# The last block's second half of tokens first, and token factors inside the last additions, in an attention and expert kernel

## The chip, the cores and the metric

The kernel runs on 1 core of one Trainium2 chip. The metric is the device time of one execution in microseconds (us); less is better. A core has a matrix engine (TensorE, PE in the rows; its weight loads are PEld), a vector engine (DVE), a scalar engine (ACT), GpSimd (POOL), and SyncE (SP), which issues transfers. Each runs its own instructions in the order in which they were written, and waits on semaphores for the others.

## What is computed

Three layers, one after the other: an attention with landmarks, a layer of eight experts of which each token takes one, and a layer with a squared ReLU. The change touches the third alone:

```python
def _moe2_ref(x, w_in, w_out):          # x: 4608 tokens x 512; w_in: 512 x 2048; w_out: 2048 x 512
    h = np.maximum(x @ w_in, 0.0)
    return (h * h @ w_out).astype(np.float32)

x = np.ascontiguousarray(attn_out.transpose(0, 2, 1, 3)).reshape(B * S, H * D)
x = _moe_ref(x=x, **moe_kwargs)
return _moe2_ref(x=x, **moe2_kwargs)
```

## The kernel before

The third layer is `phase_m2`. The 4608 tokens go in 18 blocks of `TB` = 256 (`NB` = 18), each in two halves t = 0 and t = 1 of 128 tokens. Tokens lie sorted by expert, so each block has a tile `fa` with a scale factor for each token (`sc[t]`) and the row of the output to which the token belongs.

The hidden width of 2048 is worked through in 8 pairs per block, 144 pairs in all. For one pair, `pair` issues 24 matmuls (lines 1136 to 1138, tile `h2`, shown as h) for two slices of 128 hidden columns. ACT takes the ReLU (line 1141), DVE squares (line 1142) and forms the combinations for a seven-product scheme in place of eight (Strassen's; lines 1143 to 1146), ACT rounds them to float16 (line 1148, `hq[:, 0]`), and after the `yield` DVE writes the rest that the rounding lost (line 1150, `hq[:, 1]`).

`piece(b, f)` then issues 21 matmuls (line 1158): for each of the seven products k, three matmuls (high by high, high by low, low by high), added up in PSUM over the 8 pairs of the block. The seven sums lie two and two in four PSUM tiles, `sums[k // 2][:, k % 2]`; each tile is one bank of PSUM. In the order of k the sums are called p1, p6 (tile o0), p7, p5 (o1), p4, p3 (o2) and p2 (o3).

`result(b)` makes the output of the block from the seven sums: `r[0]` = p1, `r[1]` = p6 + r0, `r[2]` = p7 + r1, the four quarters `o[t][:, z]` by further additions (line 1170, DVE), then for each t a multiplication of 128x512 elements by the token factors (line 1173, ACT, inside `put`) and an indirect DMA that POOL issues (line 1174) and that scatters 128 rows into the output. Both transfers of a block write the tensor `out`, and each waits for the one before.

The order is written out by hand, with a loop over g: at step g the kernel issues `pair` g, then `piece` of pair g - 2 (`LAG` = 2), then, where that piece is the last of a block, `result`, and then what is left of `pair` g (line 1150). So PE alternates between 24 and 21 matmuls, and the 21 matmuls of the next block, which begin the four tiles of sums anew, stand one pair behind `result`.

Of the kernel before, what the change touches and what calls it, by code (L numbers as in the profile page):

```python
# [6 lines left out]
F32 = mybir.dt.float32  # L7
# [3 lines left out]
AF = mybir.ActivationFunctionType  # L11
ALU = mybir.AluOpType
# [1084 lines left out]
TB = 256  # L1097
LAG = 2

PRODS = ((5, 5), (1, 1), (6, 6), (0, 0), (4, 2), (2, 4), (3, 3))  # L1100


def load_block(nc, pool, x2, blk):

    n = TB // 128
    xT = pool.tile([128, 8, TB], F16, tag="x2T", name="x2T")
    for t in range(n):
        r0 = TB * blk + 128 * t
        nc.sync.dma_start_transpose(out=xT[:, :, 128 * t:128 * t + 128], in_=x2[r0:r0 + 128, 0:2 * DM])
    fa = pool.tile([128, n, 4], F16, tag="fa", name="fa", bufs=3)  # L1110
    nc.sync.dma_start(out=fa, in_=x2[TB * blk:TB * blk + TB, 2 * DM:XD].rearrange("(a p) c -> p a c", p=128))
    return xT, fa


def phase_m2(tc, x2, wi, wo, first, out):


    nc = tc.nc
    V, ACT, PE = nc.vector, nc.scalar, nc.tensor
    with (  # L1120
        tc.tile_pool(name="n2", bufs=2, reuse_waits="tile") as n2,
        tc.tile_pool(name="n3", bufs=3, reuse_waits="tile") as n3,
        tc.tile_pool(name="npo", bufs=1, space=PSUM, reuse_waits="tile") as npo,
        tc.tile_pool(name="nph", bufs=4, space=PSUM, reuse_waits="tile") as nph,
    ):
        NB = NT // TB
        NP = 8 * NB
        sums = [npo.tile([128, 2, TB], F32, name=f"o{i}") for i in range(4)]

        def pair(xT, i, s):  # L1130

            ph = nph.tile([128, 2, TB], F32, tag="h2", name="h2")
            for z, f in enumerate((i + 8, i)):
                fs = slice(128 * f, 128 * f + 128)
                for c in range(4):
                    PE.matmul(ph[:, z], wi[:, 0, c, fs], xT[:, c], start=(c == 0), stop=False)  # L1136
                    PE.matmul(ph[:, z], wi[:, 0, c, fs], xT[:, 4 + c], start=False, stop=False)  # L1137
                    PE.matmul(ph[:, z], wi[:, 1, c, fs], xT[:, c], start=False, stop=(c == 3))  # L1138

            q = n3.tile([128, 7, 128], F32, tag="q", name="q")  # L1140
            ACT.activation(q[:, 3:7], ph.rearrange("p z (t n) -> p (z t) n", t=2), AF.Relu, scale=2.0 ** -7)  # L1141
            V.tensor_tensor(q[:, 3:7], q[:, 3:7], q[:, 3:7], op=ALU.mult)  # L1142
            V.tensor_tensor(q[:, 0], q[:, 6], q[:, 4], op=ALU.add)
            V.tensor_tensor(q[:, 6], q[:, 5], q[:, 6], op=ALU.subtract)
            V.tensor_tensor(q[:, 1], q[:, 0], q[:, 5], op=ALU.subtract)
            V.tensor_tensor(q[:, 2], q[:, 3], q[:, 1], op=ALU.subtract)  # L1146
            s["hq"] = hq = n3.tile([128, 2, 7, 128], F16, tag="hq", name="hq", bufs=4)
            ACT.activation(hq[:, 0], q, AF.Copy, scale=0.5)  # L1148
            yield
            V.scalar_tensor_tensor(hq[:, 1], q, 0.5, hq[:, 0], op0=ALU.mult, op1=ALU.subtract)  # L1150

        def piece(b, f):

            hq = ps[8 * b + f]["hq"]
            for k, (a, w) in enumerate(PRODS):
                for i, (u, x) in enumerate(((0, 0), (0, 1), (1, 0))):

                    PE.matmul(sums[k // 2][:, k % 2], hq[:, u, a], wo[:, x, f, w], start=(f == 0 and i == 0 and k % 2 == 0),  # L1158
                              stop=(f == 7 and i == 2), skip_group_check=True)

        def result(b):

            fa = st[b][1]
            sc = [fa[:, t, 0:2].bitcast(F32) for t in range(2)]
            o = [n2.tile([128, 2, TB], F32, tag=f"out{t}", name=f"out{t}") for t in range(2)]
            r = [n2.tile([128, TB], F32, tag=f"r{i}", name=f"r{i}") for i in range(3)]
            p1, p6, p7, p5, p4, p3, p2 = (sums[k // 2][:, k % 2] for k in range(7))

            def add(to, x, y):
                V.tensor_tensor(to, x, y, op=ALU.add)  # L1170

            def put(t):
                ACT.activation(o[t], o[t], AF.Copy, scale=sc[t])  # L1173
                nc.gpsimd.indirect_dma_start(  # L1174
                    out=out, out_offset=bass.IndirectOffsetOnAxis(ap=fa[:, t, 2:4].bitcast(I32), axis=0),
                    in_=o[t].rearrange("p z n -> p (z n)"), in_offset=None)
            ACT.activation(r[0], p1, AF.Copy)  # L1177
            add(r[1], p6, r[0])
            add(r[2], p7, r[1])
            add(o[0][:, 1], p5, r[1])  # L1180
            add(o[1][:, 1], p5, r[2])
            add(o[1][:, 0], p4, r[2])
            put(1)
            add(o[0][:, 1], p3, o[0][:, 1])
            add(o[0][:, 0], p2, r[0])
            put(0)

        st = list(first)
        ps = [{} for _ in range(NP)]
        for g in range(NP + LAG):  # L1190
            rest = iter(())
            if g < NP:
                b, i = divmod(g, 8)
                if i == 0 and len(st) < min(b + 2, NB):
                    st.append(load_block(nc, n2, x2, b + 1))
                rest = pair(st[b][0], i, ps[g])
                next(rest)
            if g >= LAG:
                piece(*divmod(g - LAG, 8))
                if (g - LAG) % 8 == 7:  # L1200
                    result((g - LAG) // 8)
            next(rest, None)


# [8 lines left out]
def moe_kernel(tc, q, k, v, wg, w1, w2, win, wout, out, x_rows, x2):  # L1213
    nc = tc.nc
    with tc.tile_pool(name="cst", bufs=1, reuse_waits="tile") as cp:
# [16 lines left out]
        with (  # L1232
# [4 lines left out]
            with tc.tile_pool(name="mb", bufs=1, reuse_waits="tile") as mb:  # L1237
# [3 lines left out]
                with tc.tile_pool(name="fp", bufs=2, reuse_waits="tile") as fp:  # L1241
                    pend = {}

                    def fill(j):

                        i = j - PT
                        if 0 <= i < 32:
# [3 lines left out]
                            else:  # L1251
# [9 lines left out]
                    phase_m1(tc, cst, x_rows, x2, w1, w2, rt, stg, wb, fill,  # L1261
                             lambda: b0.extend(load_block(nc, x0, x2, b) for b in range(1)))
            phase_m2(tc, x2, wi, wo, b0, out)


# [21 lines left out]
```

## Time and profile before

| | us |
|---|---|
| median of 3 runs | 1443.82 |
| lowest and highest | 1439.42, 1449.20 |
| the profiled execution, its own time | 1445.92 |
| its span, from the first to the last instruction | 1444.20 |
| third layer, from its first sums to the last | about 730 to 1434 |

The span of the profiled execution is 1.7 us shorter than its own time; the rest lies around it. The profiled execution is 2.1 us above the median. In the rows, times are us from the span's start unless a unit stands there; a row of a timeline gives the start, the time taken, and, in brackets, how long the engine was idle before it and what ended that.

### The profile page before, as it was taken

What the parts mean: (1) busy time and instruction counts of PE and PEld (TensorE: products, weight loads), DVE (VectorE), ACT (ScalarE), POOL (GpSimd) and SP (SyncE); (2) the same over time, 40 slices, a digit from 0 to 9 for tenths busy, and PEclk for the clock granted to TensorE, in tenths of its full rate; (3) what the DMA queues carried; (4) which work ended last, traced back from release to release, by engine and by line L of the source; (5) the groups of instructions that cost most, each with busy time, mean ns of one, the idle gap of its engine ahead of it and who ended that gap; (6) DMA issues with size and microseconds to landing.
All of it is one profiled execution on the core that took longest, in us unless ns stands there. A gap on an engine that the chain in (4) does not pass through costs nothing. (4 is left out here: it accounts for less than half of the span.)

```text
span 1444.2 us, 35176 instructions
## 1 busy us (share of the span) xinstructions
PE 1352.3 (94%) x14312; PEld 1077.5 (75%) x14312; DVE 1040.5 (72%) x2651; ACT 575.8 (40%) x979; POOL 274.1 (19%) x282
## 2 busy tenths in 40 slices
PE   5999889889898997899899999999999999999996
PEld 4555555667575775667688888888888888888886
DVE  5888998858888887989556666666666666666664
ACT  4555565333553353443333333333333333333332
POOL 4434563111111223132200000000000000000000
PEclk9999999999999999999999999999999999999999
DMA  8767674476758547364310111111111101111100
GB/s 197 164 162 187 158 175 94 122 190 126 212 119 224 131 123 205 87 132 102 72 33 16 30 31 31 30 23 24 29 30 30 30 19 27 30 31 30 30 9 22
DMA packets 133695, 127.05 MB, mean 88 GB/s; under 512 B 90832, under 2 KB 109264, under 8 KB 133520
## 3 DMA queue, kind: packets, MB, share of 16 engines
q1 hardware_dynamic: 123680, 94.45, 28.5%
q0 software_dynamic: 9200, 30.21, 6.7%
q8 instruction: 114, 1.87, 0.6%
q14 instruction: 61, 0.50, 0.1%
q10 hardware_dynamic: 640, 0.02, 0.0%
HBM read 219.49 MB, written 28.89 MB: 172 GB/s over the span
## 5 line engine op out<-in xcount | busy, mean ns | idle before, releaser
L1158 PE MATMUL o<-wo,hq 128*128 128x256 f16 x3024 | 356.1, 272 | 0.0
L1158 PEld LDWEIGHTS <-hq 128*128 128x128 f16 x3024 | 295.6, 98 | 37.3 <-issue 2.8
L1136 PE MATMUL h<-x2T,wi 128*128 128x256 f16 x1152 | 314.8, 273 | 5.0 <-ACTq L1037 5.0
L1138 PE MATMUL h<-x2T,wi 128*128 128x256 f16 x1152 | 314.7, 273 | 0.0
L1137 PE MATMUL h<-x2T,wi 128*128 128x256 f16 x1152 | 314.7, 273 | 0.0
L1148 ACT ACTIVATE hq<-q 128x896 f16<-128x896 f32 x144 | 136.8, 950 | 289.9 <-DVE q L1146 289.9
L1150 DVE SCALAR_TENSOR_TENSOR hq<-q,hq 128x896 f16<-128x896 f32 x144 | 157.1, 1091 | 129.0 <-ACT hq L1148 129.0
L135 PE MATMUL py<-wb,hT 128*128 128x512 f16 x864 | 202.3, 392 | 22.2 <-DVE ss L153 16.3
L120 PE MATMUL ph<-xT,wb 128*128 128x128 f16 x1152 | 196.9, 220 | 8.7 <-DMA xT<-xh 6.8
L122 PE MATMUL ph<-xT,wb 128*128 128x128 f16 x1152 | 196.9, 220 | 3.4 <-DVE wb L1046 3.2
L121 PE MATMUL ph<-xT,wb 128*128 128x128 f16 x1152 | 196.9, 220 | 0.0
L1174 POOL DMA_INDIRECT out<-out,fa x36 | 54.5, 1514 | 665.3 <-ACT out L1173 590.6
L135 PEld LDWEIGHTS <-hT 128*128 128x128 f16 x864 | 84.9, 101 | 124.0 <-DVE hT L126 18.2
L1142 DVE TENSOR_TENSOR q<-q 128x512 f32<-128x512 f32 x144 | 99.5, 691 | 92.6 <-ACT q L1141 92.6
L1141 ACT ACTIVATE q<-h 128x512 f32<-128x512 f32 x144 | 85.4, 593 | 139.7 <-PE h L1138 139.7
L120 PEld LDWEIGHTS <-wb 128*128 128x128 f16 x1216 | 119.6, 98 | 14.8 <-issue 3.8
L1137 PEld LDWEIGHTS <-wi 128*128 128x128 f16 x1152 | 113.0, 98 | 16.2 <-issue 2.9
L1136 PEld LDWEIGHTS <-wi 128*128 128x128 f16 x1152 | 113.0, 98 | 15.7 <-SPq L1037 2.5
L1138 PEld LDWEIGHTS <-wi 128*128 128x128 f16 x1152 | 113.0, 98 | 13.4
L122 PEld LDWEIGHTS <-wb 128*128 128x128 f16 x1216 | 119.6, 98 | 4.4 <-DVE wb L1046 4.4
L121 PEld LDWEIGHTS <-wb 128*128 128x128 f16 x1216 | 119.6, 98 | 4.0
L126 DVE SCALAR_TENSOR_TENSOR hT<-ph,hT 128x512 f16<-128x512 f32 x72 | 49.7, 690 | 61.0 <-ACT hT L125 31.0
(289 smaller groups left out, 1904.8 us busy)
## 6 DMA issues: line engine op xcount, KB each, us to landing
stg<-in_moe_w SPq DMA_DIRECT2D x76, 2048.0 KB
qn<-in_q SPq DMA_DIRECT2D x16, 576.0 KB
kn<-in_k SPq DMA_DIRECT2D x16, 576.0 KB
vn<-in_v SPq DMA_DIRECT2D x16, 576.0 KB
fw<-in_moe_w_in SPq DMA_DIRECT2D x16, 512.0 KB
fw<-in_moe_w_out SPq DMA_DIRECT2D x16, 512.0 KB
x_rows<-xr SPq DMA_DIRECT2D x32, 192.0 KB
stg<-in_moe_w SPq DMA_DIRECT2D x16, 256.0 KB
```

Source lines behind the costliest of these rows:

```text
L120: nc.tensor.matmul(ph[:, f4], wh[:, c, fs], xT[:, c], start=(c == 0), stop=False)
L121: nc.tensor.matmul(ph[:, f4], wh[:, c, fs], xT[:, 4 + c], start=False, stop=False)
L122: nc.tensor.matmul(ph[:, f4], wl[:, c, fs], xT[:, c], start=False, stop=(c == 3))
L135: self.nc.tensor.matmul(py, hT[:, a, f], w[:, f], start=(i == 0), stop=(i == len(ps) - 1))
L1136: PE.matmul(ph[:, z], wi[:, 0, c, fs], xT[:, c], start=(c == 0), stop=False)
L1137: PE.matmul(ph[:, z], wi[:, 0, c, fs], xT[:, 4 + c], start=False, stop=False)
L1138: PE.matmul(ph[:, z], wi[:, 1, c, fs], xT[:, c], start=False, stop=(c == 3))
L1141: ACT.activation(q[:, 3:7], ph.rearrange("p z (t n) -> p (z t) n", t=2), AF.Relu, scale=2.0 ** -7)
L1142: V.tensor_tensor(q[:, 3:7], q[:, 3:7], q[:, 3:7], op=ALU.mult)
L1148: ACT.activation(hq[:, 0], q, AF.Copy, scale=0.5)
L1150: V.scalar_tensor_tensor(hq[:, 1], q, 0.5, hq[:, 0], op0=ALU.mult, op1=ALU.subtract)
L1158: PE.matmul(sums[k // 2][:, k % 2], hq[:, u, a], wo[:, x, f, w], start=(f == 0 and i == 0 and k % 2 == 0), stop=(f == 7 and i == 2), skip_ ...
```

## The change

In `result`, t = 1 is finished first for every block: the additions of `o[1]` come before anything of `o[0]`, and p5 + r1 goes to a new tile `r[3]`. For t = 0, ACT multiplies `r[3]` and `r[0]` by the token factors (two instructions of 128x256), and the last two additions of DVE become multiply-and-adds that scale p3 and p2 on their way (lines 1188 and 1189). The multiplication of `o[0]` as a whole goes. A `yield` splits `result` ahead of these two.

In the last block alone, pair 143 is issued before piece 4, the pieces 5, 6 and 7 are cut into products 0 to 4 and products 5 and 6, and the second parts of all three (18 matmuls) come after the first half of `result`.

```diff
-        def piece(b, f):
+        def piece(b, f, ks=range(7)):
 
             hq = ps[8 * b + f]["hq"]
-            for k, (a, w) in enumerate(PRODS):
+            for k in ks:
+                a, w = PRODS[k]
...
             def put(t):
-                ACT.activation(o[t], o[t], AF.Copy, scale=sc[t])
                 nc.gpsimd.indirect_dma_start(
...
             add(r[2], p7, r[1])
-            add(o[0][:, 1], p5, r[1])
             add(o[1][:, 1], p5, r[2])
             add(o[1][:, 0], p4, r[2])
+            add(r[3], p5, r[1])
+            ACT.activation(o[1], o[1], AF.Copy, scale=sc[1])
             put(1)
-            add(o[0][:, 1], p3, o[0][:, 1])
-            add(o[0][:, 0], p2, r[0])
+            ACT.activation(r[3], r[3], AF.Copy, scale=sc[0])
+            ACT.activation(r[0], r[0], AF.Copy, scale=sc[0])
+            yield
+            V.scalar_tensor_tensor(o[0][:, 1], p3, sc[0], r[3], op0=ALU.mult, op1=ALU.add)
+            V.scalar_tensor_tensor(o[0][:, 0], p2, sc[0], r[0], op0=ALU.mult, op1=ALU.add)
             put(0)
...
             if g >= LAG:
-                piece(*divmod(g - LAG, 8))
-                if (g - LAG) % 8 == 7:
-                    result((g - LAG) // 8)
+                if g == NP - 2:
+
+                    next(rest, None)
+                    continue
+                if g == NP - 1:
+                    piece(NB - 1, 4)
+                b, f = divmod(g - LAG, 8)
+
+                end = b == NB - 1 and f >= 5
+                piece(b, f, range(5) if end else range(7))
+                if f == 7:
+                    res = result(b)
+                    next(res)
+                    for f in range(5, 8) if end else ():
+                        piece(b, f, (5, 6))
+                    next(res, None)
```

DVE at the end of the block before the last (block 16), before the change. The names out0 and out1 are `o[0]` and `o[1]`, o0 to o3 the four tiles of sums; each row ends with what it waits for (DMASW and DMAHW are transfers).

```order
L1170 TENSOR_TENSOR r1_22462<-o0_14413,r0_22461 128x256 [waits Activation_49]
L1170 TENSOR_TENSOR r2_22463<-o1_14414,r1_22462 128x256 [waits DVE_49,PE_49]
L1170 TENSOR_TENSOR out0_22459<-o1_14414,r1_22462 128x256 [waits DMASW7_49]
L1170 TENSOR_TENSOR out1_22460<-o1_14414,r2_22463 128x256 [waits DMASW6_49,DVE_49]
L1170 TENSOR_TENSOR out1_22460<-o2_14415,r2_22463 128x256 [waits PE_49]
L1170 TENSOR_TENSOR out0_22459<-o2_14415,out0_22459 128x256 [waits DVE_49]
L1170 TENSOR_TENSOR out0_22459<-o3_14416,r0_22461 128x256 [waits PE_49]
L1150 SCALAR_TENSOR_TENSOR hq_22436<-q_22429,hq_22436 128x896
```

The same place on DVE after the change:

```order
L1171 TENSOR_TENSOR r1_22494<-o0_14413,r0_22493 128x256 [waits Activation_49]
L1171 TENSOR_TENSOR r2_22495<-o1_14414,r1_22494 128x256 [waits DVE_49,PE_49]
L1171 TENSOR_TENSOR out1_22492<-o1_14414,r2_22495 128x256 [waits DMASW6_49,DVE_49]
L1171 TENSOR_TENSOR out1_22492<-o2_14415,r2_22495 128x256 [waits PE_49]
L1171 TENSOR_TENSOR r3_22496<-o1_14414,r1_22494 128x256
L1188 SCALAR_TENSOR_TENSOR out0_22491<-o2_14415,fa_21439,r3_22496 128x256 [waits DMAHW4_49,DMASW7_49,Activation_49]
L1189 SCALAR_TENSOR_TENSOR out0_22491<-o3_14416,fa_21439,r0_22493 128x256 [waits PE_49,Activation_49]
L1150 SCALAR_TENSOR_TENSOR hq_22468<-q_22461,hq_22468 128x896
```

The last read of tile o1 moves from the fourth place to the fifth, and the two rows that read o2 and o3 last now wait for ACT.

ACT at the same place, before the change (fa holds the token factors, q and hq belong to the pairs):

```order
L1177 ACTIVATE r0_22461<-o0_14413 128x256 [waits PE_49]
L1173 ACTIVATE out1_22460<-out1_22460,fa_21411 128x512 [waits DMAHW4_49,DMASW6_49,DVE_49]
L1173 ACTIVATE out0_22459<-out0_22459,fa_21411 128x512 [waits DMASW7_49,DVE_49]
L1141 ACTIVATE q_22502<-h2_22477 128x512 [waits PE_49,Activation_49]
L1148 ACTIVATE hq_22509<-q_22502 128x896 [waits DVE_49]
```

And after it:

```order
L1177 ACTIVATE r0_22493<-o0_14413 128x256 [waits PE_49]
L1183 ACTIVATE out1_22492<-out1_22492,fa_21439 128x512 [waits DMAHW4_49,DMASW6_49,DVE_49]
L1185 ACTIVATE r3_22496<-r3_22496,fa_21439 128x256 [waits DVE_49]
L1186 ACTIVATE r0_22493<-r0_22493,fa_21439 128x256 [waits Activation_49]
L1141 ACTIVATE q_22536<-h2_22511 128x512 [waits PE_49]
```

Ahead of the two multiply-and-adds of DVE there now stand the scaling of out1 and of r3, in this order; the second 128x512 scaling is gone.

PE after the change at the end of the last block, where the last piece's product 4 ends and product 5 of piece 5 follows (hq_22802 is that of pair 143, hq_22711 that of pair 141):

```order
L1159 MATMUL o2_14415<-wo_4552,hq_22802 128x256
L1159 LDWEIGHTS hq_22802
L1159 MATMUL o2_14415<-wo_4552,hq_22802 128x256
L1159 LDWEIGHTS hq_22711
L1159 MATMUL o2_14415<-wo_4552,hq_22711 128x256 [waits DVE_49]
L1159 LDWEIGHTS hq_22711
L1159 MATMUL o2_14415<-wo_4552,hq_22711 128x256
```

The 18 matmuls that were moved behind the first half of `result` begin with a wait for DVE; the pieces of the last block before the change have none there.

## Rows read from the trace of the kernel before

**Rows 1.** The page, part 1: busy time of each engine, share, instructions.
```profile
PE 1352.3 (94%) x14312; PEld 1077.5 (75%) x14312; DVE 1040.5 (72%) x2651; ACT 575.8 (40%) x979; POOL 274.1 (19%) x282
```
**Rows 2.** Busy time by stretch: PE, PEld, DVE, ACT, POOL, granted clock, DMA share, GB/s.
```profile
808.00:1399.00 591.00, 591.00 (x5395) 527.42 (x5393) 377.84 (x825) 206.41 (x285) 46.70 (x30) 1.00 0.12 27
```
**Rows 3.** Waits of PE's weight loads, 730 to 1434: us in all, times, longest.
```profile
PEld L1158 <- issue: 2.8, 17, 0.2
```
**Rows 4.** Timeline of PE: the first piece of block 17, in three parts.
```profile
1401.21 0.82 PE L1158 MATMUL o<-wo,hq 128*128 128x256 f16 x6
...
1402.01 0.81 PE L1158 MATMUL o<-wo,hq 128*128 128x256 f16 x6
...
1402.67 0.60 PE L1158 MATMUL o<-wo,hq 128*128 128x256 f16 x4
```
**Rows 5.** Timeline of DVE at the same place: the result of block 16.
```profile
1400.34 0.42 DVE L1170 TENSOR_TENSOR r<-o,r 128x256 f32<-128x256 f32 x1 [1.29 <-ACT r L1177]
...
1400.87 0.42 DVE L1170 TENSOR_TENSOR r<-o,r 128x256 f32<-128x256 f32 x1
1401.21 0.42 DVE L1170 TENSOR_TENSOR out<-o,r 128x256 f32<-128x256 f32 x1
...
1401.54 0.41 DVE L1170 TENSOR_TENSOR out<-o,r 128x256 f32<-128x256 f32 x1
...
1401.87 0.41 DVE L1170 TENSOR_TENSOR out<-o,r 128x256 f32<-128x256 f32 x1
1402.20 0.41 DVE L1170 TENSOR_TENSOR out<-o,out 128x256 f32<-128x256 f32 x1
```
**Rows 6.** Timeline of ACT at the same place.
```profile
1402.32 0.72 ACT L1173 ACTIVATE out<-out,fa 128x512 f32<-128x512 f32 x1 [2.01 <-DVE out L1170]
...
1402.99 0.72 ACT L1173 ACTIVATE out<-out,fa 128x512 f32<-128x512 f32 x1
...
1403.61 0.58 ACT L1141 ACTIVATE q<-h 128x512 f32<-128x512 f32 x1
```
**Rows 7.** Groups by line and shape: busy us, mean ns of one, idle before.
```profile
L1141 ACT ACTIVATE q<-h 128x512 f32<-128x512 f32 x144 | 85.4, 593 | 139.7 <-PE h L1138 139.7
...
L1173 ACT ACTIVATE out<-out,fa 128x512 f32<-128x512 f32 x36 | 24.9, 722 | 36.3 <-DVE out L1170 36.3
...
L1177 ACT ACTIVATE r<-o 128x256 f32<-128x256 f32 x18 | 6.6, 366 | 1.8 <-PE o L1158 1.8
...
L1150 DVE SCALAR_TENSOR_TENSOR hq<-q,hq 128x896 f16<-128x896 f32 x144 | 157.1, 1091 | 129.0 <-ACT hq L1148 129.0
```
**Rows 8.** Timelines of DVE, PEld and ACT at the end of the last block.
```profile
1424.79 1.09 DVE L1150 SCALAR_TENSOR_TENSOR hq<-q,hq 128x896 f16<-128x896 f32 x1 [1.01 <-ACT hq L1148]
1426.82 0.69 DVE L1142 TENSOR_TENSOR q<-q 128x512 f32<-128x512 f32 x1 [0.93 <-ACT q L1141]
...
1430.85 0.22 PEld L1158 LDWEIGHTS <-hq 128*128 128x128 f16 x3 [0.24 <-DVE hq L1150]
...
1431.50 0.38 ACT L1177 ACTIVATE r<-o 128x256 f32<-128x256 f32 x1 [1.83 <-PE o L1158]
...
1433.90 0.72 ACT L1173 ACTIVATE out<-out,fa 128x512 f32<-128x512 f32 x1 [2.01 <-DVE out L1170]
```
**Rows 9.** Timeline of POOL (blocks 16 and 17), and the chain that ended last.
```profile
1403.32 1.47 POOL L1174 DMA_INDIRECT out<-out,fa  x1 [33.73 <-ACT out L1173]
...
1436.37 0.98 POOL L1174 DMA_INDIRECT out<-out,fa  x1 [26.71 <-issue]
1439.88 0.97 POOL L1174 DMA_INDIRECT out<-out,fa  x1 [2.53 <-DMA out<-out,fa]
...
1436.37 2.73 DMA out<-out,fa
```
**Rows 10.** Busy time by stretch, columns as in rows 2: two places before the third layer's sums.
```profile
555.20:558.20 3.00, 0.34 (x2) 0.00 (x0) 2.90 (x9) 1.25 (x2) 0.00 (x0) 1.00 1.22 212
721.10:724.50 3.40, 3.37 (x17) 2.38 (x17) 0.00 (x0) 0.00 (x0) 0.00 (x0) 0.50 0.23 85
```

More of the change, by code (lines that the diff above doesn't have):

```diff
@@ L1165, in result @@
             o = [n2.tile([128, 2, TB], F32, tag=f"out{t}", name=f"out{t}") for t in range(2)]
-            r = [n2.tile([128, TB], F32, tag=f"r{i}", name=f"r{i}") for i in range(3)]
+            r = [n2.tile([128, TB], F32, tag=f"r{i}", name=f"r{i}") for i in range(4)]
             p1, p6, p7, p5, p4, p3, p2 = (sums[k // 2][:, k % 2] for k in range(7))
```

## The prediction

> **What bounds the kernel now.** The page comes first: PE is busy 94% of the span [rows 1]. An average over three layers says little, so the next view is busy time by stretch. From 808 to 1399 us, inside the third layer, PE is busy for all of 591.00 us with 5395 matmuls, 0.1095 us each, at a granted clock of 1.00 [rows 2]: one matmul starts every 0.109 us and nothing else matters as long as PE is fed. The list of waits names the exceptions: 17 times PE's loads for line 1158 were held, 2.8 us in all, 0.165 us each [rows 3]. There are 17 block ends with a block behind them, so every one of them costs a little already, and a block end is the place to read closely. In the first piece of block 17 six matmuls start from 1401.21, the seventh not at 1401.87 but at 1402.01, and the thirteenth at 1402.67 [rows 4]. The seventh opens tile o1 again. It writes the half of p7, which DVE read last in r2 (ended 1401.29), yet it starts 0.06 us after the end, at 1401.95, of the addition that read p5, the other half of that tile [rows 5]. So a piece waits at its 1st, 7th, 13th and 19th matmul for the last reader of a whole tile of sums, and at the seventh this wait decides already: **there is no slack between the result of a block and the next block's sums.** The thirteenth follows the last read of o2 (1402.20 + 0.41 = 1402.61 [rows 5]) by the same 0.06 us, so it has none either.
>
> The Trainium skill, "PSUM — Partial Sum Buffer", section "PSUM bank collisions raise a hardware error", says that an engine which reads a bank while a matmul writes any part of it collides, so software has to keep them apart. The row of the seventh matmul agrees: the half does not count, the tile does.
>
> **The change at the 17 block ends.** The first half of `result` is the same up to r2, which starts at 1400.87. Then the order differs. Before, p5 + r1 needed no r2 and began 0.34 us later; now the first addition of out1 comes next and needs r2, so it starts when r2 has ended and been signalled. From DVE to ACT a signal takes 0.04 us (an addition ends at 1402.28, ACT starts at 1402.32 [rows 5, 6]); I take the same inside DVE: 1400.87 + 0.42 + 0.04 = 1401.33. Independent additions follow each other by 0.33 us [rows 5]: second addition of out1 1401.66 to 1402.07, r3 1401.99 to 1402.40. r3 is now the last reader of o1, so the seventh matmul starts at 1402.46 and not at 1402.01: **0.45 us** later.
>
> For o2, DVE's multiply-and-add of p3 waits for ACT's scaled r3, and ACT does out1 first. ACT starts on out1 at 1402.07 + 0.04 = 1402.11, and the next instruction starts 0.67 us behind a 128x512 one (1402.32, 1402.99 [rows 6]): r3 at 1402.78. How long 128x256 takes from SBUF with a factor per token is in no row. It lies between 0.366 us (that size, from PSUM, no factor) and 0.722 us (twice the size, with the factor); 512 instead of 256 elements from PSUM cost 0.593 - 0.366 = 0.227 us, so I take 0.722 - 0.227 = 0.495 us [rows 7]. It ends at 1403.27, DVE starts at 1403.31. A multiply-and-add of 896 elements takes 1.09 us [rows 7], an addition of 256 takes 0.42 [rows 5]; at one element rate for both that is 0.42 us here: end 1403.73, and the thirteenth matmul at 1403.79, where it was 1402.67. That is **1.12 us** in all, 0.45 of it already waited at the seventh. The nineteenth needs o3: scaled r0 follows on ACT from about 1403.22 to 1403.71, DVE's last multiply-and-add runs 1403.75 to 1404.17, and PE comes to it at 1403.79 + 6 x 0.109 = 1404.44; nothing is added.
>
> Nobody gives this back. PE has no idle time later to absorb it [rows 2]. Behind the waiting DVE instruction stand line 1150 of the pair under way, and behind that the squares of the next pair. Line 1150 moves to about 1404.1 and ends at 1405.2; its hq is read a pair and a piece after 1401.21, some 45 x 0.109 = 4.9 us, so from 1406.1 at the earliest: hidden, with 0.9 us to spare. ACT's line 1141, at 1403.61 [rows 6], comes at about the same time, since one scaling of 128x512 becomes two of 128x256. Where an output leaves costs nothing in the first 17 blocks: POOL idles 33.7 us ahead of the next [rows 9]. Sum: 17 x 1.12 = **+19.0 us**; with 0.366 or 0.722 us for the unknown scaling the thirteenth matmul stands at 1403.66 or 1404.01, 0.99 or 1.34 us late: +16.8 to +22.8.
>
> **The change at the end.** Pair 143 goes ahead of piece 4, 21 x 0.109 = 2.3 us earlier on PE, but its squares stand on DVE behind line 1150 of pair 142, which ends at 1424.79 + 1.09 = 1425.88; line 1142 can come at 1425.87 and not 1426.82, 0.95 us earlier [rows 8]. From there to the end of the last hq nothing changes, and the last piece waited for just that (PEld 1430.85, 0.24 us for line 1150 [rows 8]), so its sums are 0.95 us earlier, and r0 starts at 1430.55 in place of 1431.50. Then r1, r2 and the two additions of out1 as above: r0 + 2.15 us to the end of out1, against 1433.90 - 1431.50 = 2.40 us to ACT's start on it before. ACT starts on out1 at about 1432.73, **1.17 us earlier**. The 18 matmuls moved back must wait for the same addition, since p3 shares a tile with p4: they run from 1432.75 to 1434.9, and out0 is ready at about 1435.4.
>
> That lateness is hidden by POOL. The first transfer began at 1436.37 and landed 2.73 us later, and only then the second started, at 1439.88 [rows 9]. The second start moves with the first, and out0 has until about 1438. In the last block the first transfer began 1.75 us after ACT's end on out1 (1434.62); in block 16 it was 0.28 us (1403.04 to 1403.32) [rows 6, 8, 9]. If the 1.75 stays, the end moves by -1.2 us; with 0.28 by -2.6; if DVE's work beside it stretches POOL's instruction from 0.98 to 1.47 us as in block 16 [rows 9], by -0.7. I take **-1.2**, the nearest row being that of the same transfer.
>
> **Sum.** +19.0 - 1.2 = +17.8 us, bounds 16.8 - 2.6 = +14.2 and 22.8 - 0.7 = +22.1. The profiled execution took 1445.9 us (span 1444.2 and 1.7 around it), so this one would take 1463.7; it lay 2.1 us above the median of the runs, and against 1443.8 the time is **1461.6 us**, 1.2% more.
>
> **Rivals.**
> The block ends cost nothing and only the end of the program is seen: 1443.8 - 1.2 = 1442.6. The mechanism would be slack: PE reaching the seventh and thirteenth matmul after 1402.40 and 1403.73 anyway. It decides if the first piece of the next block came 1.1 us later against DVE. The pause of 0.14 us at 1401.87 and the 17 equal pauses speak against it [rows 3, 4]; for it speaks only that rows of PE are partly modelled. 0.07.
>
> The halves of a tile are waited for apart. Then the seventh goes free after r2, the tenth (p5) waits for r3 until 1402.46 (0.27 us later than 1401.21 + 9 x 0.109), and the sixteenth (p3), before at 1402.67 + 0.33 = 1403.00, starts at 1403.79: 0.79 us, 17 x 0.79 - 1.2 = +12.2, 1456.0. The seventh matmul's row speaks against it. The rule of the Trainium skill's page on PSUM named above would exclude it altogether; by halves the sum would be 1456.0, by whole banks 1461.6. 0.08.
>
> The pauses lower the clock. After a wait of 5.0 us a stretch of 3.4 us ran at 0.50, the level of 1.2 GHz in place of 2.4 [rows 10]. Were that to follow each block end, it would cost about 1.7 us more each, 17 x 1.7 = 29: 1490. The Trainium skill, "TensorE: Matmul & The Clock Gate", Part 1, takes the low clock for the default and activity for what lifts it, which makes such a fall possible. But a stretch at 555 us with two matmuls in 3 us kept 1.00 [rows 10], and pauses of 0.45 and 0.67 us are far shorter. 0.03.
>
> **Chances.** The forecast has 0.80, and 0.02 is left for what I don't see. About 1% (14.4 us) is what a measurement of this kernel can tell from no change: three runs lay between 1439.4 and 1449.2. The forecast lies only 3.4 us beyond that line, so of its 0.80 some 0.13 fall within 1%, and 0.67 are slower; with the clock rival 0.70. The first two rivals are within 1%: 0.07 + 0.08 + 0.13 = 0.28, of which the first could reach -1% by scatter alone; faster 0.02. The range for 8 in 10 takes the bounds (1458 to 1466) with the scatter of a median, and reaches down past the rival of the halves: 1453 to 1468.
>
> **What would show it.** Right: at each of 17 block ends PE pauses about 0.6 us ahead of the seventh matmul of a piece (0.15 before) and about 0.65 us ahead of the thirteenth, ended by DVE, while DVE waits some 0.9 us for ACT in `result`; the list of waits has 20 us on these lines; the first transfer of the last block starts about 1.2 us earlier against the last pair. Wrong: no pause ahead of the thirteenth, or the transfers of the last block not moved, or a granted clock under 1.00 after 735 us.

## The result, and the profile after

| | before | after |
|---|---|---|
| median, lowest to highest, 6 runs each (us) | 1448.12, 1439.42 to 1449.77 | 1465.9, 1462.85 to 1469.94 |
| ratio of after to before, 95% interval | | 1.0136, 1.0111 to 1.0161 |
| profiled execution, its span (us) | 1445.92, 1444.2 | 1466.19, 1464.5 |

The changed kernel is 1.4% slower; 17.8 us had been forecast, the medians differ by 17.8 us, and the spans of the two profiled executions by 20.3 us. The median of before rose from 1443.8 to 1448.1 us when three more runs joined it, so the forecast of 1461.6 us, made against the first three, lies 4.3 us below the median of after for that reason alone. That the 17.8 us of the forecast and those of the medians agree to 0.1 us is luck: the interval of the ratio leaves 16 to 23 us. The traces, added up below, give 19.3 - 1.24 = 18.1 us for the change itself.

The page, part 1, of the kernel after (busy time, share, instructions) tells almost nothing apart from [rows 1]; the work is the same:

```profile
PE 1354.6 (92%) x14312; PEld 1078.6 (74%) x14312; DVE 1045.4 (71%) x2651; ACT 578.2 (39%) x997; POOL 255.5 (17%) x282
```

Only ACT has 18 instructions more, one per block. The list of waits from 730 us to the end (us in all, times, longest) is where to look:

```profile
PEld L1159 <- issue: 23.9, 35, 1.4
...
DVE out L1188 <- ACT r L1185: 14.6, 17, 0.9
PE o L1159 <- DVE out L1188: 9.0, 17, 0.5
PE o L1159 <- DVE r L1171: 7.6, 17, 0.5
```

Before there were 2.8 us in 17 waits of the weight loads and no such wait of PE's matmuls [rows 3]. Now 17 waits end with r (the new last reader of o1) and 17 with the multiply-and-add of p3 (the last reader of o2), and ahead of the second DVE itself waits 17 times, 0.86 us each, for ACT. The weight loads' waits are the same pauses seen from the other side, longer, since a matmul's modelled end hides some 0.17 us of each: 23.9 us now in 35 waits, 1.4 of it at the end of the program.

The timeline of PE at the first piece of block 17, in three parts as in [rows 4], with the idle time ahead in brackets:

```profile
1421.60 0.82 PE L1159 MATMUL o<-wo,hq 128*128 128x256 f16 x6
...
1422.87 0.81 PE L1159 MATMUL o<-wo,hq 128*128 128x256 f16 x6 [0.45 <-DVE r L1171]
...
1424.21 0.38 PE L1159 MATMUL o<-wo,hq 128*128 128x256 f16 x2 [0.53 <-DVE out L1188]
```

The seventh matmul starts 1.27 us behind the first (0.80 before, by the rows) and the thirteenth 2.61 (1.46 before). DVE and ACT at the same place, against [rows 5] and [rows 6]:

```profile
1421.27 0.42 DVE L1171 TENSOR_TENSOR r<-o,r 128x256 f32<-128x256 f32 x1
1421.73 0.42 DVE L1171 TENSOR_TENSOR out<-o,r 128x256 f32<-128x256 f32 x1
...
1422.07 0.41 DVE L1171 TENSOR_TENSOR out<-o,r 128x256 f32<-128x256 f32 x1
1422.40 0.41 DVE L1171 TENSOR_TENSOR r<-o,r 128x256 f32<-128x256 f32 x1
1423.67 0.48 DVE L1188 SCALAR_TENSOR_TENSOR out<-o,fa,r 128x256 f32<-128x256 f32 x1 [0.86 <-ACT r L1185]
1424.07 0.48 DVE L1189 SCALAR_TENSOR_TENSOR out<-o,fa,r 128x256 f32<-128x256 f32 x1
```

```profile
1422.52 0.72 ACT L1183 ACTIVATE out<-out,fa 128x512 f32<-128x512 f32 x1 [1.81 <-DVE out L1171]
1423.15 0.49 ACT L1185 ACTIVATE r<-r,fa 128x256 f32<-128x256 f32 x1
1423.55 0.49 ACT L1186 ACTIVATE r<-r,fa 128x256 f32<-128x256 f32 x1
```

r3 ends at 1422.81 and PE goes on at 1422.87; the multiply-and-add of p3 ends at 1424.15 and PE goes on at 1424.21. Both times 0.06 us lie between, as before the change.

The end of the program, timelines of PE, DVE, ACT and POOL, against [rows 8] and [rows 9]:

```profile
1439.93 0.27 PE L1136 MATMUL h<-x2T,wi 128*128 128x256 f16 x1
...
1451.37 1.59 PE L1159 MATMUL o<-wo,hq 128*128 128x256 f16 x13 [0.25 <-DVE hq L1150]
1454.22 2.13 PE L1159 MATMUL o<-wo,hq 128*128 128x256 f16 x18 [1.27 <-DVE out L1171]
...
1456.53 0.47 DVE L1189 SCALAR_TENSOR_TENSOR out<-o,fa,r 128x256 f32<-128x256 f32 x1
...
1452.01 0.38 ACT L1177 ACTIVATE r<-o 128x256 f32<-128x256 f32 x1 [1.83 <-PE o L1159]
1454.21 0.72 ACT L1183 ACTIVATE out<-out,fa 128x512 f32<-128x512 f32 x1 [1.81 <-DVE out L1171]
...
1456.67 0.98 POOL L1174 DMA_INDIRECT out<-out,fa  x1 [28.71 <-ACT r L1186]
1460.18 0.97 POOL L1174 DMA_INDIRECT out<-out,fa  x1 [2.52 <-DMA out<-out,fa]
```

A yardstick for the end alone is the stretch from pair 142's first matmul, the last thing that is the same in both, to the start of the last transfer. Before, that matmul starts here:

```profile
1418.39 0.27 PE L1136 MATMUL h<-x2T,wi 128*128 128x256 f16 x1
```

That is 1439.88 - 1418.39 = 21.49 us before and 1460.18 - 1439.93 = 20.25 us after: 1.24 us are won, and then the first transfer's landing stands ahead of the second as it did.

**Where the 20.3 us of the spans came from.** For the block ends the yardstick is the first transfer of block 0 and of block 16 on POOL:

```profile
774.02 0.97 POOL L1174 DMA_INDIRECT out<-out,fa  x1 [50.71 <-ACT out L1183]
...
1423.52 0.97 POOL L1174 DMA_INDIRECT out<-out,fa  x1 [36.11 <-ACT out L1183]
```

649.50 us for 16 blocks, 40.59 each; before, 772.03 to 1403.32 is 631.29 us, 39.46 each. So a block end costs 1.14 us more, and 17 of them 19.3 us. The end gives back 1.24. The rest, 2.2 us, arose before the change has any effect: the first matmul of line 1159 starts at 732.8 us, that of line 1158 at 730.6.

### The profile page after: what moved, and what is told of

It reads as the page before. It is cut to its first block, busy times and chain, and to the rows that moved or that the text cites. A ratio compares the mean times of both kernels' runs of the same rounds, so it can differ in the third digit from the quotient of the medians.

```text
span 1464.5 us, 35163 instructions
## 1 busy us (share of the span) xinstructions
PE 1354.6 (92%) x14312; PEld 1078.6 (74%) x14312; DVE 1045.4 (71%) x2651; ACT 578.2 (39%) x997; POOL 255.5 (17%) x282
## 5 line engine op out<-in xcount | busy, mean ns | idle before, releaser
L1159 PE MATMUL o<-wo,hq 128*128 128x256 f16 x3024 | 358.9, 272 | 18.1 <-DVE out L1188 9.0
L1159 PEld LDWEIGHTS <-hq 128*128 128x128 f16 x3024 | 295.6, 98 | 58.4 <-issue 23.9
L1174 POOL DMA_INDIRECT out<-out,fa x36 | 35.6, 989 | 702.2 <-ACT out L1183 626.4
```

## The experiments

The columns of this table are read from the trace of each kernel: the distance of blocks (first transfers of blocks 0 and 16, over 16), the seventh and thirteenth matmul of a block's first piece behind its first, and the stretch from pair 142 to the last transfer. All are taken before rounding, those of the matmuls as medians over the 17 block ends. The last column is the ratio to the kernel before, with its 95% interval; e6, e7 and e8 ran once and have none.

| kernel | distance | seventh | thirteenth | end stretch | ratio |
|---|---|---|---|---|---|
| before | 39.46 | 0.81 | 1.47 | 21.49 | |
| after | 40.59 | 1.27 | 2.61 | 20.25 | 1.0136 (1.0111 to 1.0161) |
| e1_tail_only | 39.45 | 0.80 | 1.46 | 20.25 | 0.9984 (0.9961 to 1.0008) |
| e2_ends_only | 40.59 | 1.26 | 2.60 | 21.27 | 1.0119 (1.0064 to 1.0175) |
| e3_both_orders | 39.52 | 0.80 | 1.53 | 20.25 | 0.9973 (0.9948 to 0.9998) |
| e4_act_order | 40.31 | 1.26 | 2.32 | 20.26 | 1.0096 (1.0067 to 1.0125) |
| e5_dve_order | 40.80 | 0.81 | 2.81 | 20.26 | 1.0166 (1.0119 to 1.0212) |
| e6_split_alone | 39.46 | 0.81 | 1.47 | 21.27 | |
| e7_act_goes_on | 39.46 | 0.81 | 1.47 | 20.26 | |
| e8_pair_alone | 39.46 | 0.81 | 1.47 | 21.14 | |
| e9_pool_goes_on | 39.46 | 0.81 | 1.47 | 20.26 | 1.0018 (0.9993 to 1.0042) |

The theory: PE, which has no slack, waits at each block end for the last reader of a whole tile of sums, and the change makes these readers late. The main rival, once the result was known: the instructions that the change adds cost by themselves, or the cut last block does.

### The two halves of the change apart: e1 and e2

e1_tail_only gives blocks 0 to 16 their old result back and leaves the last block as changed:

```diff
             add(r[2], p7, r[1])
+            if b < NB - 1:
+                add(o[0][:, 1], p5, r[1])
+                add(o[1][:, 1], p5, r[2])
+                add(o[1][:, 0], p4, r[2])
+                ACT.activation(o[1], o[1], AF.Copy, scale=sc[1])
+                put(1)
+                add(o[0][:, 1], p3, o[0][:, 1])
+                add(o[0][:, 0], p2, r[0])
+                ACT.activation(o[0], o[0], AF.Copy, scale=sc[0])
+                put(0)
+                yield
+                return
```

> Blocks 0 to 16 take the old result, block 17 the changed order and the split pieces. Theory (all of the loss is PE held at the 17 block ends by tiles of sums that are read later; the end of the program gains): the distance from one block's first sums to the next goes back from 40.59 to 39.46 us, and the stretch from pair 142's first matmul to the end of the span stays at 24.57 us as after the change (25.81 before): 1.2 us less than before, which is less than a time of the whole can tell. Rival (something else in the changed program, such as the split last block, also costs in every block or before the third layer): distances above 39.46, or a time more than 5 us above before.

The distances are those of before and the end stretch is that of after. The time, 0.9984 of before, is not told apart from no change, as a gain of 1.2 us in 1446 (0.1%) can't be.

e2_ends_only keeps the changed result and takes the cuts and the early pair away:

```diff
-                if g == NP - 2:
-
-                    next(rest, None)
-                    continue
-                if g == NP - 1:
-                    piece(NB - 1, 4)
...
-                end = b == NB - 1 and f >= 5
+                end = False
```

> The changed result in all 18 blocks, the last block's pieces and pair 143 in the old order. Theory: 17 x 1.14 = 19.4 us from the block ends, and of the end's gain only the part that the order of out1 gives (r0 to ACT's start on out1 2.15 to 2.2 us in place of 2.40), about -0.2 us: +19.2 us against before, end stretch 25.6 us. Rival (the slowdown belongs to the split last block): the time of before, distances 39.46.

It has the distances of after and an end stretch 0.22 us below before; its ratio covers both +19.2 us (1.013) and after. So all of the loss sits in the code of `result`, and none in the cut last block.

### The same instructions in another order: e3, e4, e5

All three keep every instruction of the change and the last block as changed. In blocks 0 to 16, e4_act_order moves two lines of ACT, e5_dve_order one line of DVE, and e3_both_orders both, so that it reads:

```diff
             add(r[2], p7, r[1])
+            add(r[3], p5, r[1])
             add(o[1][:, 1], p5, r[2])
             add(o[1][:, 0], p4, r[2])
-            add(r[3], p5, r[1])
-            ACT.activation(o[1], o[1], AF.Copy, scale=sc[1])
-            put(1)
             ACT.activation(r[3], r[3], AF.Copy, scale=sc[0])
             ACT.activation(r[0], r[0], AF.Copy, scale=sc[0])
+            ACT.activation(o[1], o[1], AF.Copy, scale=sc[1])
+            put(1)
             yield
```

> Same instructions as after the change, block 17 in the order of the change; in blocks 0 to 16 DVE adds r3 ahead of out1, and ACT scales r3 and r0 ahead of out1. Theory (what counts is when the last reader of a tile of sums is done, not how many instructions there are): seventh matmul as before; r3 scaled 1.32 to 1.81 us after r1's start, multiply-and-add of p3 ends 2.34 us after r1's start, thirteenth matmul 0.05 to 0.1 us later than before: distance 39.5 to 39.55, about +1 us in 17 ends, with the end's -1.2 about the time of before. Rival (the two more ACT instructions, the 0.06 us longer multiply-and-adds and the wait on ACT cost by themselves): the distance stays near 40.59, +18 us.

Timelines of e3_both_orders at the first piece of block 16, PE and then DVE:

```profile
1362.88 0.82 PE L1159 MATMUL o<-wo,hq 128*128 128x256 f16 x6
1363.69 0.81 PE L1159 MATMUL o<-wo,hq 128*128 128x256 f16 x6
1364.41 0.49 PE L1159 MATMUL o<-wo,hq 128*128 128x256 f16 x3
```

```profile
1362.02 1.28 DVE L1171 TENSOR_TENSOR r<-o,r 128x256 f32<-128x256 f32 x3 [1.29 <-ACT r L1177]
1363.22 0.74 DVE L1171 TENSOR_TENSOR out<-o,r 128x256 f32<-128x256 f32 x2
1363.88 0.48 DVE L1197 SCALAR_TENSOR_TENSOR out<-o,fa,r 128x256 f32<-128x256 f32 x1
```

DVE waits for ACT no longer, and the thirteenth matmul is 0.06 us later than before (1.53 against 1.47). With the same instructions as after the loss falls from 1.14 us per block end to 0.06, so the rival of the instructions' own cost is out. What they do cost is at most that 0.06 us.

> As after the change, but in blocks 0 to 16 ACT scales r3 and r0 ahead of out1; DVE's order is that of the change. Theory: the seventh matmul stays 0.45 us late (r3 is still the last reader of its tile); r3 is scaled from 2.1 to 2.6 us after r1's start, the multiply-and-add of p3 ends at 3.1, the thirteenth matmul 0.83 us late in place of 1.14: distance 40.28, 14.1 us in 17 ends, +12.9 us in all. Rival (halves of a tile waited for apart, or one single wait behind the loss): no change of the distance against 40.59, or all of it gone.

The distance is 40.31 us where 40.28 was expected: r3 still keeps the seventh matmul 0.45 us late, and the multiply-and-add of p3 comes 0.29 us sooner than after the change.

> As after the change, but in blocks 0 to 16 DVE adds r3 ahead of out1; ACT's order is that of the change, out1 first. Theory: the seventh matmul is back at its old place, yet out1 is complete 0.2 us later, ACT starts on it later, scales r3 after it, and the thirteenth matmul comes 1.34 us late in place of 1.14: distance of the blocks 40.79 us, 17 x 1.34 - 1.2 = +21.5 us, slower than the change itself although one of its two waits is gone. Rival (the two waits are separate losses that add up): 0.45 us less per block end than after the change, distance 40.14, +10.5 us.

Timeline of PE in e5_dve_order at the same place:

```profile
1380.48 0.82 PE L1159 MATMUL o<-wo,hq 128*128 128x256 f16 x6
1381.29 0.82 PE L1159 MATMUL o<-wo,hq 128*128 128x256 f16 x6
1383.29 0.49 PE L1159 MATMUL o<-wo,hq 128*128 128x256 f16 x3 [1.19 <-DVE out L1197]
```

The first wait is gone and the second has grown by more than that: 40.80 us per block, slower than the change. The two waits do not add up. They are two checks of one chain, and only the later one counts; the earlier merely takes part of its price in advance.

### The parts of the gain at the end: e6 and e8

Both start from e1_tail_only. e6_split_alone takes the early pair 143 away (the first six lines removed in e2), e8_pair_alone the cuts (the last line changed in e2).

> Old result in blocks 0 to 16; in block 17 the changed result and the split pieces, but pair 143 in its old place behind piece 4. Theory (the last hq, on DVE, gates the last piece): the last piece's third matmul can't start before line 1150 of pair 143 has ended, where it did before the change, so r0 comes no earlier and only the order of out1 gains: end stretch 25.6 us (25.81 before, 24.57 after). Rival (the 18 matmuls moved back, 2.0 us, are what is won): end stretch below 24.6.

> Old result in blocks 0 to 16; in block 17 the changed result and pair 143 ahead of piece 4, but no piece is cut. Theory: PE ends with the same 84 matmuls in a row, without the 0.24 us wait for the last hq, and out1's order gives its 0.2: end stretch 25.3 us. Rival (moving the pair is what wins 0.95): 24.8 or less.

Timeline of PE at the last piece of e6_split_alone:

```profile
1429.57 0.39 PE L1159 MATMUL o<-wo,hq 128*128 128x256 f16 x2 [0.36 <-ACT hq L1148]
1430.69 1.59 PE L1159 MATMUL o<-wo,hq 128*128 128x256 f16 x13 [0.73 <-DVE hq L1150]
```

And of e8_pair_alone, up to the end of its last piece:

```profile
1428.81 4.31 PE L1159 MATMUL o<-wo,hq 128*128 128x256 f16 x38
```

With the cuts alone PE reaches the last piece early and waits there for its hq, so r0 starts 13.11 us behind pair 142's first matmul, as before the change: the stretch wins 0.22 us. With the early pair alone the hq is as early as after the change, but PE has all 84 matmuls of the last four pieces to do and reaches the last of them, without a pause, hardly earlier than before; r0 starts at 12.97, and the stretch wins 0.35 of the 0.5 us expected. Most of these two gains is the order of out1, which e2 has alone (0.22): against e2 (21.27) the cuts add nothing (21.27), the early pair 0.13 (21.14), and both together 1.02 (20.25). So the cuts are of use only with the early pair, and the early pair is worth little without them. (The spans of e1, e6 and e7 end 0.16 us later behind the last transfer, 4.47 us and not 4.31, which is why the expectations, made in spans, read 0.16 us off; behind that of e9 stand its memsets.)

### A lag that stayed open: e7 and e9

The first transfer of the last block starts 1.75 us behind ACT's end on out1 before the change (1434.62 to 1436.37) and after it (1454.93 to 1456.67), and 0.28 us in the other blocks (1423.24 to 1423.52). Two attempts at the cause, both on e1_tail_only:

```diff
             put(0)
+            if b == NB - 1:
+                for _ in range(6):
+                    ACT.activation(r[1], r[2], AF.Copy)
```

> As e1_tail_only, with six more instructions of ACT behind the last result (128x256 copies of r2 into r1, which nothing reads). It asks why the first transfer of the last block starts 1.75 us after ACT's end on out1 and 0.28 us in the other blocks. Theory (an ACT that comes to the end of its program signals late): the lag falls to about 0.3 us and the end stretch from 24.7 to about 23.3. Rival (the lag is POOL's own): the lag stays 1.75, end stretch 24.6 to 24.8.

```diff
             put(0)
+            if b == NB - 1:
+                z = n2.tile([128, 8], F32, tag="z", name="z")
+                for _ in range(30):
+                    nc.gpsimd.memset(z, 0.0)
```

> As e1_tail_only, with 30 small memsets of POOL (128x8, a tile that nothing reads) behind the last transfer. It asks again where the 1.75 us between ACT's end on out1 and the first transfer of the last block come from, now that ACT's end of program is excluded. Theory (POOL close to the end of its own program is late): the lag falls to about 0.3 us as in the other blocks, and the transfers of the last block come 1.5 us earlier against pair 142; what the memsets take behind them may show at the end. Rival (it hangs on something else in the last block): lag 1.75 us. The time of the whole can't tell either way; the distances of blocks stay 39.46.

ACT's and POOL's timelines in e9_pool_goes_on:

```profile
1429.84 0.72 ACT L1195 ACTIVATE out<-out,fa 128x512 f32<-128x512 f32 x1 [1.81 <-DVE out L1171]
...
1432.31 0.98 POOL L1174 DMA_INDIRECT out<-out,fa  x1 [25.39 <-ACT r L1198]
```

1430.56 to 1432.31 is 1.75 us again, and e7 has 1.75 as well (ACT ends at 1437.43, POOL starts at 1439.18). Both theories fell: neither ACT's nor POOL's end of program is the cause. Nor is it a transfer: in none of the eleven traces is a DMA packet under way within the lag, one that loads instructions included. The cause stays open.

## Why the prediction was right, point by point

- **PE is the bound and has no slack at a block end.** Right. What delays the thirteenth matmul delays everything: 1.14 us there, 1.14 us per block, to the last block.
- **The seventh matmul, +0.45 us.** Measured 0.46. r3, moved to the fifth place on DVE, is the last reader of o1; e5 put it back to the third and the wait went.
- **The thirteenth matmul, +1.12 us.** Measured 1.14. The parts: ACT's scaling of r3, bounded by 0.366 and 0.722 us and taken as 0.495, took 0.492. The Trainium skill, "ScalarE: Activation LUTs", section "What ACT_TABLE_LOAD costs", gives 280 ns and 0.833 ns per element for an instruction with a bias for each partition, and 93 ns as the share of each operand of that kind. The factor here is one such operand, which makes 493 ns as an estimate for 256 elements, and the trace agrees (492). The multiply-and-add was taken as long as an addition (0.42) and took 0.48; ACT's step behind out1 was taken as 0.67 and is 0.63. The two errors nearly cancel. 17 x 1.14 = 19.3 against 19.0 forecast.
- **A tile is waited for as a whole.** Right. With halves waited for apart the seventh matmul, which writes the half of p7, would not have waited for r3, which reads p5; it did in all 17 places, and the sum of that rival (+12.2 us) did not come. What is shown is a wait that the program carries (a semaphore of DVE). Each tile of sums is one bank, so no run tells tile from bank, and none lets the matmul go on without the wait.
- **Nothing else is late.** Right: line 1150 is no wait of PE at the block ends, and the granted clock from 774 to 1452 us is 1.00, with pauses of 0.6 and 0.7 us in the stretch.
- **The end, -1.2 us.** Measured 1.24: r0 starts 1.03 us earlier against pair 142, and out1's order gives 0.20 (2.40 to 2.20 us from r0 to ACT's start on out1). The step named holds in part: the last hq is ready 1.02 us earlier (0.95 forecast) and gates the last piece, but the prediction gave all of this to the early pair and did not ask whether PE would be there in time. It is there only because the cuts take 18 matmuls out of its way; without them (e8) the early hq brings r0 0.14 us and not 1.03. The 18 matmuls moved back waited 1.27 us for the addition of p4, as forecast, and out0, ready at 1457.0, still waited for the first transfer's landing. The lag of 1.75 us stayed, as the nearest row had it.
- **The rival in which the block ends cost nothing** fell with the 34 waits.

## What to carry to other kernels

When an engine is busy without a gap, look at what it waits for at the seams, however short the wait: a pause of 0.14 us says that there is no slack, and that each step put ahead of its releaser is paid in full, here 17 times for a gain that is had once. Order the readers of a shared accumulator so that those which free it come first, and put no instruction of a second engine into that chain if something else stands ahead of it in that engine's queue; e3 shows that the same instructions cost 0.06 or 1.14 us, by their order alone. A reorder meant for the last iteration belongs in the last iteration.

## What the runs showed that I had not expected

- POOL's record of the first transfer of a block is 1.47 us long in blocks 0 to 16 of before, e1, e3, e4 and e6 to e9, and 0.97 us in after, e2 and e5; the second transfers of before lie between 0.97 and 1.75. The 396 records of the eleven traces show what goes with it, the DVE instruction under way when POOL starts. In block 16 of before that is line 1150, which reads two tiles outside PSUM, q and hq:

```profile
1402.87 1.08 DVE L1150 SCALAR_TENSOR_TENSOR hq<-q,hq 128x896 f16<-128x896 f32 x1
```

  It ends at 1403.95 and POOL's record at 1404.79 [rows 9], 0.84 us later. So it is, to within 0.84 to 0.85 us, in all 258 records that start with over 0.15 us of line 1150 left, whatever is left of it. Where DVE is idle at POOL's start, as in after, or in a multiply-and-add that reads a tile of sums, the record is 0.97 to 0.98 us (85 records). No run varied this alone. It cost nothing here, since in the lists of waits no engine but POOL itself waits for these transfers.
- The scatter of the times arises before the third layer: its first sums start between 727.8 us (e9) and 737.7 us (e4) in the profiled executions, while the distance of blocks agrees to 0.01 us among the kernels that should share it. Distances within one trace tell effects of 0.06 us per block apart which the medians can't: by its trace e3 should win 0.2 us (17 x 0.06 lost, 1.24 won), but its ratio of 0.9973 stands for 3.9 us, and the interval leaves out 1.
- The lag of 1.75 us ahead of the first transfer of the last block, the same to 0.01 us in all eleven kernels, has no cause that I could show.
